# A decayed linear attention and a maxout feed-forward: from nested periods to one written list of steps

## The chip, the cores and the metric

The kernel runs on one core of a Trainium2 chip. Its engines are TensorE (PE; its weight loads are a row of their own, PEld), VectorE (DVE), ScalarE (ACT), GpSimd (POOL) and SyncE (SP), which here only issues DMAs. Each engine takes its instructions in the order in which the program writes them. The metric is the device time of one execution in microseconds, as the median of several runs.

## What is computed

An attention with a state that decays per channel (`S` is 768 steps, 8 heads of 48 channels, batch 4), and then a feed-forward whose hidden value is the larger of two projections (width 1024):

```python
for t in range(S):
    cur = einsum('bhd,bhe->bhde', u * k[t], v[t])
    y[t] = einsum('bhd,bhde->bhe', r[t], state + cur)
    state = w[t][..., None] * state + einsum('bhd,bhe->bhde', k[t], v[t])
x = y.transpose(0, 2, 1, 3).reshape(B * S, H * D)
out = np.maximum(x @ w1, x @ w2) @ w_out
```

The term of `cur` is called the bonus here: for each step and head it is v times the sum of r·k·u over the channels.

## The kernel before

The sequence is cut into six chunks of 128 steps, and a unit is one chunk of two batch entries (called halves, b = 0 and 1): 12 units in all, `units` in line 41, with the two pairs of batch entries in turn. A unit depends on the state that the same pair left a chunk earlier, two units before.

Attention of a unit: `log_w` (L122) takes the logarithm of w on ACT, `excl` (L132) sums it along the chunk on TensorE with a triangular matrix, and `incl` (L133, VectorE), `Aex` (L137, ACT) and `Ainv` (L164, ACT) are made from that sum. `scaled_r` and `scaled_k` (L168, L171, VectorE) multiply r and k with them. `transposes` (L198) turn both on TensorE into one PSUM tile `tp`, copied out by ACT for half 0 and by VectorE for half 1 (L206, L208); `scores` (L217) multiplies them into `mt_p`, and `mask` (L222, VectorE) takes the triangle into `MTm`. `y_sum` adds the part from the state (L236) and that of the chunk (L240) to the tile `y_p`.

The bonus goes ahead of that: `bonus_k` (L175, GpSimd) makes k·u, `bonus_r` (L181, VectorE) multiplies by r, `bonus_sum` (L185, VectorE) reduces to `dg`, and `bonus_out` (L229, VectorE) writes v·dg into `y_p`, for each half, before the matmuls that add to it. One matmul at the start (L85) marks the tile so that all later ones add. There is one `y_p`, one `ex_p`, one `tp` and one `mt_p` (two banks); `kv_p` and the transposed x share a bank, and the feed-forward has two. After `y_sum`, ACT copies out `xs` (L246), `x_transposes` (L253) turns it, VectorE copies `xT` (L257). The state is added up by `state_sum` (L268), `state_out` (L277, L279 on VectorE, L284 on GpSimd), with a decay that goes through DRAM (`row` L143, back as `Wt` L150, exponential `Wx` L159).

Feed-forward: the larger of a and b is half of (a + b) plus half of |a − b|. So the weights are prepared once: the difference w1 − w2 (`wd_sb`, L323, VectorE), the sum (L322, GpSimd), which is transposed (L328) and multiplied with w_out (`prep_product`, L334). `hidden` (L295) multiplies x with the difference in four steps of six matmuls, and ACT takes the absolute value (L298); `rows_out` adds x times the product (L304, three matmuls) and the absolute value times w_out (L308, eight) for each half, and `store` copies out and stores (L314, L316).

The order is written by hand. `start()` runs attention 0, the preparation and hidden 0; then `period(i, j, f, more)` interleaves attention of unit i, the preparation of r and k of unit j = i + 1, the feed-forward of unit f = i − 1, and the loads of unit i + 2. All DMAs go through SP's queue: four loads of 384 KB a unit (w, k, r, v; three buffers each), two weight loads of 512 KB for each of three row blocks, w_out, u, the decay's row and the stores.

Of the kernel before, what the change touches and what calls it, by code (L numbers as in the profile page):

```python
# [12 lines left out]
AX = mybir.AxisListType  # L13


@with_exitstack
def kernel(
# [77 lines left out]
    wof = const.tile([C, FO, HD], F32)  # L95

    def load_w12():
        for ko in range(KO):
            nc.sync.dma_start(out=w1f[:, ko, :], in_=moe_w1[ko * C:(ko + 1) * C, :])
            nc.sync.dma_start(out=w2f[:, ko, :], in_=moe_w2[ko * C:(ko + 1) * C, :])  # L100

    def load_wo():
        nc.sync.dma_start(out=wof, in_=moe_w_out.rearrange("(o p) n -> p o n", p=C))

    def load(i):
        c, bp = units[i]
        sl = bass.ds(c * C, C)
        t = {}
        for name, src in (("w", w), ("k", k), ("r", r), ("v", v)):
# [20 lines left out]
    def excl(i, b):  # L130
        ex_p = ps.tile([C, HD], F32, tag="ex")
        nc.tensor.matmul(ex_p, triU, flat(st[i]["lw"][:, b]))  # L132
        nc.vector.tensor_add(flat(st[i]["incl"][:, b]), ex_p, flat(st[i]["lw"][:, b]))  # L133
        st[i]["ex", b] = ex_p

    def a_excl(i, b):
        nc.scalar.activation(flat(st[i]["Aex"][:, b]), st[i].pop(("ex", b)), AF.Exp)  # L137

    def chunk_decay_row(i):
        if units[i][0] == NC - 1:  # L140
            return
        row = dram.tile([1, NB * HD], F32)
        nc.sync.dma_start(out=row, in_=st[i]["incl"][C - 1:C].rearrange("o b h d -> o (b h d)"))  # L143
        st[i]["row"] = row

    def chunk_decay(i):
        if units[i][0] == NC - 1:
            return
        for ab in range(2):
# [5 lines left out]
    def chunk_decay_exp(i):
        if units[i][0] == NC - 1:
            return
        Wx = work.tile([C, NB, PR], F32)
        nc.scalar.activation(Wx, Wts[i % 2], AF.Exp)  # L159
        st[i]["Wx"] = Wx  # L160

    def a_inv(i):
        Ainv = work.tile([C, NB, H, D], F32)
        nc.scalar.activation(Ainv, st[i]["incl"], AF.Exp, scale=-1.0)  # L164
        st[i]["Ainv"] = Ainv

    def scaled_r(i):
        nc.vector.tensor_mul(rps[i % 2][:, :, :, 0:D], tiles[i]["r"], st[i]["Aex"])  # L168

    def scaled_k(i):  # L170
        nc.vector.tensor_mul(kps[i % 2][:, :, :, 0:D], tiles[i]["k"], st[i]["Ainv"])  # L171

    def bonus_k(i):
        ku = work.tile([C, NB, HD], F32)
        nc.gpsimd.tensor_mul(ku, tiles[i]["k"].rearrange("p b h d -> p b (h d)"),  # L175
                             u_b.unsqueeze(1).to_broadcast([C, NB, HD]))
        st[i]["ku"] = ku

    def bonus_r(i):
        ku = st[i]["ku"]  # L180
        nc.vector.tensor_mul(ku, tiles[i]["r"].rearrange("p b h d -> p b (h d)"), ku)  # L181

    def bonus_sum(i):
        dg = work.tile([C, NB * H, 1], F32)
        nc.vector.reduce_sum(dg, st[i]["ku"].rearrange("p b (h d) -> p (b h) d", d=D), axis=AX.X)  # L185
        st[i]["dg"] = dg

    def cast_v(i):
        vb = work.tile([C, NB, H, D], BF16)
        nc.gpsimd.tensor_copy(vb, tiles[i]["v"])  # L190
        st[i]["vb"] = vb


    def transposes(i, b):
        tp = ps.tile([C, 2, PR, C], BF16, tag="tp")
# [5 lines left out]
        st[i]["tp", b] = tp  # L201

    def transposes_out(i, b):
        rkT = work.tile([C, 2, PR, C], BF16, bufs=3)
        if b == 0:
            nc.scalar.copy(rkT, st[i].pop(("tp", b)))  # L206
        else:
            nc.vector.tensor_copy(rkT, st[i].pop(("tp", b)))  # L208
        st[i]["rkT", b] = rkT

    def scores(i, b):
        rkT = st[i]["rkT", b]
        mt_p = ps.tile([C, 2, PR, C], F32, tag="mt")
# [4 lines left out]
        st[i]["mt", b] = mt_p  # L218

    def mask(i, b):  # L220
        MTm = work.tile([C, 2, PR, C], BF16, bufs=3)
        nc.vector.tensor_mul(  # L222
            MTm.rearrange("p a q c -> p (a q) c"),
            st[i].pop(("mt", b)).rearrange("p a q c -> p (a q) c"),
            triU.unsqueeze(1).to_broadcast([C, H, C]))
        st[i]["MTm", b] = MTm

    def bonus_out(i, b):
        nc.vector.tensor_mul(y_p.rearrange("p (h d) -> p h d", d=D), tiles[i]["v"][:, b],  # L229
                             st[i]["dg"][:, b * H:(b + 1) * H].to_broadcast([C, H, D]))  # L230

    def y_sum(i, b):
        c, bp = units[i]
        if c > 0:
            for p in range(PR):
                nc.tensor.matmul(y_p[:, 2 * p * D:2 * (p + 1) * D], st[i]["rkT", b][:, 0, p, :],  # L236
                                 S_z[bp][:, b, p].rearrange("p a d -> p (a d)"),
                                 start=False, stop=False, skip_group_check=True)
        for h in range(H):
            nc.tensor.matmul(y_p[:, h * D:(h + 1) * D], st[i]["MTm", b][:, h % 2, h // 2, :],  # L240
                             st[i]["vb"][:, b, h, :], start=False, stop=(h == H - 1),
                             skip_group_check=True)

    def y_out(i, b):
        xs = work.tile([C, HD], BF16, bufs=3)
        nc.scalar.copy(xs, y_p)  # L246
        st[i]["xs", b] = xs

    def x_transposes(i, b):
        if b == 0:  # L250
            st[i]["xt"] = ps.tile([C, KO, NB, C], BF16, tag="kv", name="xt_p")
        for j in range(KO):
            nc.tensor.transpose(st[i]["xt"][:, j, b, :], st[i]["xs", b][:, j * C:(j + 1) * C], ident)  # L253

    def x_out(i):
        xT = mlp.tile([C, KO, NB, C], BF16, bufs=3)
        nc.vector.tensor_copy(xT, st[i].pop("xt"))  # L257
        st[i]["xT"] = xT

    def state_sum(i):  # L260
        if units[i][0] == NC - 1:
            return
        kv_p = ps.tile([C, NB, PR, D], F32, tag="kv")
        for b in range(NB):
            for p in range(PR):
                for a in range(2):
                    h = 2 * p + a
                    nc.tensor.matmul(kv_p[a * DP:(a + 1) * DP, b, p, :], kps[i % 2][:, b, h, :],  # L268
                                     st[i]["vb"][:, b, h, :])
# [17 lines left out]
    def hidden(i, f2):  # L287
        xT = st[i]["xT"]
# [231 lines left out]
```

## Time and profile before

| what | us |
|---|---|
| median of 3 runs (182.97 to 183.9) | 183.27 |
| the profiled execution | 183.35 |
| its span in the profile | 181.6 |
| ACT busy | 95.0 |
| GpSimd busy | 65.7 |
| GpSimd waiting for k to land | 40.7 |

Idle time on an engine that isn't the bottleneck costs nothing, and the busy time of TensorE counts pipelined matmuls, so that a row near 100% isn't yet an engine at its peak. A group's row gives its count, then its busy time and the mean duration of one in ns, then the idle time ahead of it and what ended that. "93.25 0.66 PE g_p L295 x6" in the chain is start, duration and what, merged over six instructions.

### The profile page before, as it was taken

Reading aid. Unit: us, or ns where it says so; the run is one execution under the profiler, and the core shown is the slowest. Engines: PE = TensorE matmul, PEld = TensorE weight load, DVE = VectorE, ACT = ScalarE, POOL = GpSimd, SP = SyncE. Lnnn points to the kernel's source line nnn. Section 1 sums busy time; section 2 is a strip of 40 time slices with the busy share of each in tenths; the row PEclk is TensorE's granted clock in tenths of the full one; section 3 lists DMA queues with packets and bytes.
Section 4 is the critical chain, followed back from the end, with each engine's and each line's share of the span. In section 5 each row is a group of like instructions: output and inputs, shape, how many; then the busy total and the mean of one; then the engine's idle time right before and its main releaser. Section 6 shows DMA issues by size and latency. Waiting matters only on the chain.

```text
span 181.6 us, 3831 instructions
## 1 busy us (share of the span) xinstructions
PE 151.1 (83%) x1537; PEld 101.8 (56%) x1537; DVE 130.1 (72%) x172; ACT 95.0 (52%) x171; POOL 65.7 (36%) x63
## 2 busy tenths in 40 slices
PE   0643376997677799999999999999999999999992
PEld 0212274554444467666667676666666766767661
DVE  2157896568389869979799797997979979747100
ACT  2222153555523474746847478465685656655351
POOL 8219914108344305054450454505545145000000
PEclk9999999999699699999999999999999999999999
DMA  5979999979929805968949779597795981020112
GB/s 116 234 251 418 379 210 178 196 147 166 185 44 214 178 4 112 224 147 175 220 96 230 157 141 226 120 224 168 144 213 118 207 191 50 0 90 0 44 46 87
DMA packets 112614, 28.82 MB, mean 159 GB/s; under 512 B 107594, under 2 KB 111818, under 8 KB 112596
## 3 DMA queue, kind: packets, MB, share of 16 engines
q1 hardware_dynamic: 112596, 28.58, 71.0%
q8 instruction: 12, 0.20, 0.5%
q14 instruction: 6, 0.05, 0.1%
HBM read 23.82 MB, written 4.75 MB: 157 GB/s over the span
## 4 chain that ended last, share of the span: by engine, by line
PE 55%; DVE 25%; issue 6%; ACT 4%; DMA 4%; SPq 3%; POOL 1%; ACTq 0%; DVEq 0%; POOLq 0%
PE o_p L308 14%; PE ex_p L132 8%; PE g_p L295 8%; DVE MTm L222 8%; PE o_p L304 6%; DVE y_p L229 5%; PE mt_p L217 4%; DMA u_b<-in_u_dram 4%; DVE ku L181 3%; PE tp L198 3%; SPq L111 3%; PE y_p L236 3%; PE y_p L240 3%; PE wc_p L334 2%; PE kv_p L268 2%
## 5 line engine op out<-in xcount | busy, mean ns | idle before, releaser
L175 POOL TENSOR_TENSOR ku<-kt,u_b 128x768 f32<-128x768 f32 x12 | 24.4, 2031 | 48.2 <-DMA kt<-in_k_dram 40.7
L295 PE MATMUL g_p<-xT,wd_sb 128*128 128x256 bf16 x288 | 40.9, 282 | 0.0
L308 PE MATMUL o_p<-wo_sb,gT 128*128 128x384 bf16 x192 | 37.9, 332 | 0.0
L298 ACT ACTIVATE gT<-g_p 128x512 bf16<-128x512 f32 x48 | 28.5, 597 | 8.9 <-PE g_p L295 8.3
L222 DVE TENSOR_TENSOR MTm<-mt_p,triU 128x1024 bf16<-128x1024 f32 x24 | 29.3, 1220 | 4.8 <-PE mt_p L217 4.3
L132 PE MATMUL ex_p<-lw,triU 128*128 128x384 f32 x48 | 23.3, 571 | 10.2 <-ACT lw L122 6.4
L284 POOL CAST sz<-sf 48x384 bf16<-48x384 f32 x20 | 18.0, 898 | 35.8 <-DVE sf L279 32.8
L295 PEld LDWEIGHTS <-wd_sb 128*128 128x128 bf16 x288 | 26.8, 100 | 5.6 <-issue 1.4
L314 ACT COPY osb<-o_p 128x384 f32<-128x384 f32 x24 | 11.5, 479 | 30.6 <-PE o_p L308 30.6
L308 PEld LDWEIGHTS <-gT 128*128 128x128 bf16 x192 | 18.7, 100 | 11.7 <-issue 1.0
L133 DVE TENSOR_TENSOR incl<-ex_p,lw 128x384 f32<-128x384 f32 x24 | 13.2, 550 | 12.1 <-PE ex_p L132 12.1
L246 ACT CAST xs<-y_p 128x384 bf16<-128x384 f32 x24 | 11.5, 480 | 19.3 <-PE y_p L240 12.9
L137 ACT ACTIVATE Aex<-ex_p 128x384 f32<-128x384 f32 x24 | 11.8, 493 | 16.6 <-DVE incl L133 16.6
L257 DVE COPY xT<-xt_p 128x768 bf16<-128x768 bf16 x12 | 6.7, 557 | 15.0 <-PE xt_p L253 15.0
L304 PE MATMUL o_p<-wc_sb,xT 128*128 128x384 bf16 x72 | 16.2, 334 | 0.0
L181 DVE TENSOR_TENSOR ku<-rt,ku 128x768 f32<-128x768 f32 x12 | 14.5, 1204 | 2.0 <-POOL ku L175 2.0
L132 PEld LDWEIGHTS ex_p<-lw,triU 128*128 128x128 f32 x48 | 7.8, 205 | 14.3 <-ACT Aex L137 7.5
L240 PE MATMUL y_p<-vb,MTm 128*128 128x48 bf16 x192 | 9.2, 188 | 7.5 <-DVE MTm L222 4.0
L229 DVE TENSOR_TENSOR y_p<-vt,dg 128x384 f32<-128x384 f32 x24 | 15.2, 635 | 0.1
L206 ACT COPY rkT<-tp 128x1024 bf16<-128x1024 bf16 x12 | 12.1, 1012 | 3.2 <-PE tp L198 3.2
L240 PEld LDWEIGHTS <-MTm 128*128 128x128 bf16 x192 | 7.6, 99 | 8.5 <-DVE MTm L222 6.8
L198 PE MATMUL tp<-ident,rp 128*128 128x128 bf16 x96 | 9.8, 228 | 2.5 <-DVE rp L168 2.5
(49 smaller groups left out, 205.6 us busy)
## 6 DMA issues: line engine op xcount, KB each, us to landing
wt<-in_w_dram SPq DMA_DIRECT2D x12, 384.0 KB
kt<-in_k_dram SPq DMA_DIRECT2D x12, 384.0 KB
rt<-in_r_dram SPq DMA_DIRECT2D x12, 384.0 KB
vt<-in_v_dram SPq DMA_DIRECT2D x12, 384.0 KB
out_dram<-osb SPq DMA_DIRECT2D x24, 192.0 KB
w1f<-in_moe_w_dram SPq DMA_DIRECT2D x3, 512.0 KB
w2f<-in_moe_w_dram SPq DMA_DIRECT2D x3, 512.0 KB
wof<-in_moe_w_out_dram SPq DMA_DIRECT2D x1, 1536.0 KB
```

What stands on the lines that cost most here:

```text
L132: nc.tensor.matmul(ex_p, triU, flat(st[i]["lw"][:, b]))
L175: nc.gpsimd.tensor_mul(ku, tiles[i]["k"].rearrange("p b h d -> p b (h d)"), u_b.unsqueeze(1).to_broadcast([C, NB, HD]))
L181: nc.vector.tensor_mul(ku, tiles[i]["r"].rearrange("p b h d -> p b (h d)"), ku)
L198: nc.tensor.transpose(tp[:, q, p, :], src[:, b, 2 * p:2 * p + 2, :].rearrange("p h d -> p (h d)"), ident)
L222: nc.vector.tensor_mul(MTm.rearrange("p a q c -> p (a q) c"), st[i].pop(("mt", b)).rearrange("p a q c -> p (a q) c"), triU.unsqueeze(1).to ...
L229: nc.vector.tensor_mul(y_p.rearrange("p (h d) -> p h d", d=D), tiles[i]["v"][:, b], st[i]["dg"][:, b * H:(b + 1) * H].to_broadcast([C, H, D]))
L240: nc.tensor.matmul(y_p[:, h * D:(h + 1) * D], st[i]["MTm", b][:, h % 2, h // 2, :], st[i]["vb"][:, b, h, :], start=False, stop=(h == H - 1 ...
L284: nc.gpsimd.tensor_copy(S_z[bp][rows, :, :, a, :], S_f[bp][rows])
L295: nc.tensor.matmul(g_p[:, q, :], wd_sb[:, ko, fo * C:(fo + 1) * C], xT[:, ko].rearrange("p b c -> p (b c)"), start=(ko == 0), stop=(ko == ...
L298: nc.scalar.activation(st[i]["gT"][:, f2 * 2:f2 * 2 + 2, :], g_p, AF.Abs)
L304: nc.tensor.matmul(st[i]["o", b], st[i]["xT"][:, ko, b, :], wc_sb[:, ko, :], start=(ko == 0), stop=False)
L308: nc.tensor.matmul(st[i]["o", b], st[i]["gT"][:, fo, b * C:(b + 1) * C], wo_sb[:, fo, :], start=False, stop=(fo == FO - 1))
```

## The change

The two functions `start` and `period` give way to one string, `ORDER`, of steps for the whole program. A step is a name with the unit and, where there is one, the half or part: `T.3.1` is the transposes of unit 3, half 1. A short loop calls the function of each step in turn, so the string is the order of every engine's queue at once. The names: `ld*` loads (`ldw12` a block of w1 and w2, `ldwo` w_out), `lw ex incl aex ainv` the decay, `rp kp` scaled r and k, `T TO` transposes and their copy out, `M MO` scores and mask, `Y YO` the sum and its copy out, `X XO` x transposed and copied, `K sa sm sb` the state, `row wt wx` its decay, `H HO` hidden and its absolute value, `O1 O2 OO st` the output, its copy and the store, `wsum wdif wT wTO wp wpO` the preparation of the weights.

In the list the feed-forward of a unit comes one to two units behind its attention, and prefix sums (`ex`) run up to two units ahead. Input buffers go from three to four, and other buffers grow.

What is computed moves too. `rku` (k·u·r) is on GpSimd instead of VectorE. `bv` (v times dg) is made on GpSimd in SBUF, and `YO` on VectorE adds it where y leaves PSUM, in place of ACT's copy; the sum in PSUM starts without the bonus and without the seeding matmul. `XO`, the copy of the transposed x, goes from VectorE to ACT. w_out is loaded by a DMA on GpSimd's queue that converts to bfloat16 on the way, in place of a load on SP's and a scaling on ACT; the half goes into `HO` and `wpO`. The first state is copied instead of added to a cleared tile.

```diff
+ORDER = """
+ldw.0 ldw.1 ldk.0 ldu ldr.0 ldw12.2 ldv.0 ldw12.0 lw.0 ex.0.0 incl.0.0 aex.0.0 ex.0.1 incl.0.1 ainv.0 row.0
+ldw.2 ldw12.1 ldr.1 ldk.1 ku.0 aex.0.1 kp.0 lw.1 ex.1.0 rp.0 rku.0 T.0.0 TO.0.0 wsum.2 aex.1.0 M.0.0 T.0.1
+MO.0.0 TO.0.1 vb.0 dg.0 M.0.1 Y.0.0 wT.2 incl.1.0 bv.0 MO.0.1 ex.1.1 wdif.2 wsum.0 YO.0.0 lw.2 wdif.0 X.0.0
+Y.0.1 aex.1.1 incl.1.1 ldwo YO.0.1 row.1 ldv.1 ldw.3 wt.0 wdif.1 ldk.2 X.0.1 ldr.2 wsum.1 ex.2.0 ldw.4 XO.0
+wT.0 wTO.2 aex.2.0 ainv.1 wTO.0 H.0.0 incl.2.0 H.0.1 HO.0.0 rp.1 K.0 HO.0.1 H.0.2 kp.1 ku.1 wT.1 HO.0.2 ex.2.1
+sa.0 T.1.0 wTO.1 H.0.3 rku.1 TO.1.0 incl.2.1 wp.0 wt.1 row.2 ldv.2 ldk.3 HO.0.3 ldr.3 T.1.1 wpO.0 dg.1 M.1.0
+aex.2.1 vb.1 wp.2 MO.1.0 bv.1 K.1 wpO.2 wp.1 sa.1 lw.3 TO.1.1 ainv.2 Y.1.0 ex.3.0 YO.1.0 wpO.1 aex.3.0
+incl.3.0 X.1.0 M.1.1 ku.2 wx.0 kp.2 O1.0.0 MO.1.1 O2.0.0 rku.2 ex.3.1 sm.0 OO.0.0 Y.1.1 rp.2 aex.3.1 O1.0.1
...
+Y.5.1 OO.3.0 ex.8.0 row.7 wx.4 st.2.0 YO.5.1 st.2.1 ldk.8 H.4.0 ldv.7 ldr.8 rku.6 OO.3.1 T.6.0 incl.8.0 wt.6
+st.3.0 HO.4.0 X.5.0 st.3.1 sm.4 H.4.1 TO.6.0 X.5.1 H.4.2 HO.4.1 dg.6 M.6.0 vb.6 HO.4.2 T.6.1 aex.8.0 MO.6.0
+H.4.3 sb.4 XO.5 ex.8.1 HO.4.3 TO.6.1 H.5.0 incl.8.1 bv.6 H.5.1 HO.5.0 M.6.1 HO.5.1 H.5.2 MO.6.1 aex.8.1 Y.6.0
...
+H.9.3 HO.9.2 bv.11 sm.9 M.11.0 HO.9.3 O1.9.0 MO.11.0 vb.11 O1.9.1 TO.11.1 sb.9 O2.9.0 X.10.1 M.11.1 OO.9.0
+O2.9.1 XO.10 st.9.0 Y.11.0 OO.9.1 H.10.0 YO.11.0 st.9.1 H.10.1 MO.11.1 HO.10.0 X.11.0 HO.10.1 H.10.2 Y.11.1
+HO.10.2 H.10.3 YO.11.1 O1.10.0 HO.10.3 X.11.1 O2.10.0 XO.11 O1.10.1 OO.10.0 st.10.0 O2.10.1 H.11.0 OO.10.1
+st.10.1 H.11.1 HO.11.0 H.11.2 HO.11.1 H.11.3 HO.11.2 O1.11.0 HO.11.3 O2.11.0 O1.11.1 OO.11.0 st.11.0 O2.11.1
+OO.11.1 st.11.1
+"""
...
-    inp = tc.alloc_tile_pool(name="inp", bufs=3)
+    inp = tc.alloc_tile_pool(name="inp", bufs=4)
     work = tc.alloc_tile_pool(name="wrk", bufs=2)
-    mlp = tc.alloc_tile_pool(name="mlp", bufs=2)
+    mlp = tc.alloc_tile_pool(name="mlp", bufs=3)
...
-    y_p = ps.tile([C, HD], F32)
-    nc.tensor.matmul(y_p, ident, S_z[0].rearrange("p b q a d -> p (b q a d)")[:, 0:HD])
...
+    def ldwo():
+        nc.gpsimd.dma_start(out=wo_sb, in_=moe_w_out.rearrange("(o p) n -> p o n", p=C))
...
+    def wpO(ko):
+        nc.scalar.mul(wc_sb[:, ko, :], st.pop(("wp", ko)), 0.5)
...
-    def bonus_r(i):
-        ku = st[i]["ku"]
-        nc.vector.tensor_mul(ku, tiles[i]["r"].rearrange("p b h d -> p b (h d)"), ku)
...
+    def rku(i):
+        nc.gpsimd.tensor_mul(st["ku", i], st["r", i].rearrange("p b h d -> p b (h d)"), st["ku", i])
...
+    def bv(i):
+        x = work.tile([C, NB, HD], F32, tag="bv", name="bv")
+        nc.gpsimd.tensor_mul(x.rearrange("p b (h d) -> p (b h) d", d=D),
+                             st["v", i].rearrange("p b h d -> p (b h) d"),
+                             st["dg", i].to_broadcast([C, NB * H, D]))
+        st["bv", i] = x
...
-    def bonus_out(i, b):
-        nc.vector.tensor_mul(y_p.rearrange("p (h d) -> p h d", d=D), tiles[i]["v"][:, b],
-                             st[i]["dg"][:, b * H:(b + 1) * H].to_broadcast([C, H, D]))
...
+        y_p = ps.tile([C, HD], F32, tag="y", name="y_p")
         for h in range(H):
+            nc.tensor.matmul(y_p[:, h * D:(h + 1) * D], st["MTm", i, b][:, h % 2, h // 2, :],
+                             st["vb", i][:, b, h, :], start=(h == 0), stop=(c == 0),
                              skip_group_check=True)
...
-    def y_out(i, b):
-        xs = work.tile([C, HD], BF16, bufs=3)
-        nc.scalar.copy(xs, y_p)
...
+    def YO(i, b):
+        x = work.tile([C, HD], BF16, tag="xs", name="xs", bufs=4)
+        nc.vector.tensor_add(x, st.pop(("y", i, b)), st["bv", i][:, b])
+        st["xs", i, b] = x
...
+    def XO(i):
+        x = mlp.tile([C, KO, NB, C], BF16, tag="xT", name="xT", bufs=8)
+        nc.scalar.copy(x, st.pop(("xt", i)))
...
+        if c == 0:
+            nc.vector.tensor_copy(x, kv)
+        else:
+            nc.vector.tensor_add(x, kv, x)
...
+    def HO(i, f2):
+        nc.scalar.activation(st["gT", i][:, f2 * 2:f2 * 2 + 2, :], st.pop(("g", i, f2)), AF.Abs, scale=0.5)
...
     with tc.manual_schedule():
-        start()
-        for i in range(1, n + 1):
-            period(i if i < n else None, i + 1 if i + 1 < n else None, i - 1,
-                   i + 2 if i + 2 < n else None)
+        for step in ORDER.split():
+            name, *at = step.split(".")
+            ops[name](*(int(x) for x in at))
```

More of the change, by code (lines that the diff above doesn't have):

```diff
@@ L57 @@
     u_b = const.tile([C, HD], F32)
-    rps, kps = [], []
+    rps, kps, Wts = [], [], []
     for i in range(2):
@@ L94 @@
     w2f = const.tile([C, KO, d_ff], F32)
[L95 to L109, printed above, removed]
+    st = {}
@@ L130, in excl @@
[L130 to L149, printed above, removed]
+                out=x, in_=src[bp * NB:(bp + 1) * NB, :, c * C:(c + 1) * C, :].rearrange("b h s d -> s b h d"))
+            st[name, i] = x
+        return fn
+    def lw(i):
+        x = work.tile([C, NB, H, D], F32, tag="lw", name="lw")
+        nc.scalar.activation(x, st["w", i], AF.Ln)
+        st["lw", i] = x
+    def ex(i, b):
+        ex_p = ps.tile([C, HD], F32, tag="ex", name="ex_p")
+        nc.tensor.matmul(ex_p, triU, flat(st["lw", i][:, b]))
+        st["ex", i, b] = ex_p
@@ L153, in chunk_decay @@
                 allow_slow_non_contiguous=True)
[L155 to L168, printed above, removed]
@@ L225, in mask @@
             triU.unsqueeze(1).to_broadcast([C, H, C]))
-        st[i]["MTm", b] = MTm
-    def bonus_out(i, b):
-        nc.vector.tensor_mul(y_p.rearrange("p (h d) -> p h d", d=D), tiles[i]["v"][:, b],
-                             st[i]["dg"][:, b * H:(b + 1) * H].to_broadcast([C, H, D]))
-    def y_sum(i, b):
-        c, bp = units[i]
[L234 to L238, printed above, removed]
+        st["MTm", i, b] = x
```

409 lines of the change are left out of this document (164 added, 245 removed).

## The prediction

> **What bounds it now.** I read the page first, then the stretches, then the chain in order of time. The page:
>
> ```profile
> span 181.6 us, 3831 instructions
> PE 151.1 (83%) x1537; PEld 101.8 (56%) x1537; DVE 130.1 (72%) x172; ACT 95.0 (52%) x171; POOL 65.7 (36%) x63
> PE   0643376997677799999999999999999999999992
> GB/s 116 234 251 418 379 210 178 196 147 166 185 44 214 178 4 112 224 147 175 220 96 230 157 141 226 120 224 168 144 213 118 207 191 50 0 90 0 44 46 87
> ```
>
> The PE digits are 9 from slice 16 on and 3 to 7 before it. The average of 83% is two regimes, so I cut the span at the starts of the periods:
>
> ```profile
> core 0: us, PE busy (x) PEld busy (x) DVE busy (x) ACT busy (x) POOL busy (x), PEclk, DMA share, GB/s
> 0.00:13.00 13.00, 4.24 (x10) 1.55 (x11) 3.91 (x6) 3.84 (x5) 5.04 (x16) 1.00 0.85 190
> 13.00:30.00 17.00, 8.14 (x93) 6.61 (x94) 14.02 (x14) 5.37 (x5) 12.58 (x6) 1.00 1.04 320
> 30.00:44.70 14.70, 13.08 (x87) 7.74 (x85) 8.54 (x14) 7.59 (x15) 4.06 (x6) 1.00 0.87 160
> 44.70:57.60 12.90, 10.36 (x98) 6.26 (x98) 8.83 (x12) 5.45 (x10) 6.13 (x5) 0.87 0.73 145
> 57.60:69.60 12.00, 9.58 (x94) 6.14 (x92) 9.53 (x14) 5.36 (x11) 1.93 (x2) 0.86 0.52 111
> 69.60:81.30 11.70, 11.43 (x132) 7.95 (x131) 10.40 (x15) 7.42 (x14) 4.76 (x5) 1.00 0.83 171
> 138.70:150.20 11.50, 11.29 (x132) 7.81 (x130) 10.26 (x15) 7.42 (x14) 4.78 (x5) 1.00 0.84 174
> ```
>
> From 81.3 us on a period takes 11.5 us, with TensorE busy 11.29 and VectorE 10.26: there is little to win. Before 81.3, TensorE was busy 4.24 + 8.14 + 13.08 + 10.36 + 9.58 + 11.43 = 56.8 us; 24.5 us were idle. Why it starts so late stands in the chain (start, duration, what):
>
> ```profile
> 6.26 6.66 DMA u_b<-in_u_dram
> 13.06 1.81 POOL ku L175
> 14.90 1.55 DVE ku L181
> ...
> 17.47 1.60 DVE y_p L229
> ...
> 29.52 1.41 PE g_p L295 x6
> ...
> 35.96 4.07 PE wc_p L334 x24
> ```
>
> The bonus of unit 0 sits ahead of its first output sum: u lands, GpSimd multiplies, VectorE multiplies, reduces and writes y_p, and only then may TensorE add to it. The feed-forward of unit 0 starts at 29.5.
>
> **Part by part: TensorE's work and the early stage (A).** The matmuls stay as they are, except that the seeding one goes. What they cost once warm, in the same chain:
>
> ```profile
> 24.52 0.87 PE tp L328 x8
> ...
> 93.25 0.66 PE g_p L295 x6
> 93.91 0.65 PE ex_p L132 x2
> ...
> 100.03 0.49 PE o_p L304 x3
> ...
> 103.01 1.30 PE o_p L308 x8
> ```
>
> A unit's feed-forward is 4 × 0.66 + 2 × (0.49 + 1.30) = 6.2 us; the rest of the 11.29, attention, is 5.1. By 81.3 the kernel has done feed-forward 0 to 2 (18.6), attention 0 to 3 (20.4), the prefix sums of unit 4 (2 × 0.65 = 1.3), three weight transposes (2.6) and three products (4.1): 47.0 us. Stage A asks when the new list has done as much.
>
> Its hidden sums of unit 0 need all w1 and w2. Ahead of the last block SP issues six 393 KB tensors, u and two more blocks, with that block 5.7 MB. By the GB/s digits (4.54 us each) the old kernel had moved 4.6 MB at 18.2 us and 6.35 MB at 22.7, so 21 to 23 us; some five more for VectorE's difference of the last block, what stands ahead of it in its queue and the copy of x put H.0.0 at about 28, against 29.5. By then the list has placed attention 0 without its state sum (4.7), the prefix sums of unit 1 and half of unit 2 (1.95) and two weight transposes (1.7): 8.4 us. Of 47.0, 38.6 are left. At the share of the old steady period (11.29/11.5 = 0.98) they take 39.4 us and A ends at 67.4; at that of 30.0 to 81.3 (44.45 of 51.3, or 0.87) 44.4 us and 72.4. I take **70, so 11.3 us off**: feed-forward may now fill attention's waits, but single units still make up the first ten microseconds of it.
>
> Can the loads keep up? The landings of the old kernel show where GpSimd waited for them:
>
> ```profile
> 27.92 2.12 POOL L175 TENSOR_TENSOR ku<-kt,u_b 128x768 f32<-128x768 f32 x1 [4.36 <-DMA kt<-in_k_dram]
> 31.98 0.82 POOL L190 CAST vb<-vt 128x768 bf16<-128x768 f32 x1 [1.94 <-DMA vt<-in_v_dram]
> 46.70 1.81 POOL L175 TENSOR_TENSOR ku<-kt,u_b 128x768 f32<-128x768 f32 x1 [1.41 <-DMA kt<-in_k_dram]
> ```
>
> v of unit 1 lands at 32, k of unit 3 at 46.7: 8 to 10 us a unit, and a period moves a unit's loads and stores in a DMA share of 0.84 of 11.5 = 9.7 us. So v arrives about 33, 43, 52 and 62 for units 1 to 4. Attention 3 has to be through at 70, so loads are ahead by ten microseconds. On SP, stores wait for their output copy and loads queue behind them, as before; four input buffers instead of three give a unit more of slack. I cost that at nothing; uncovered, a late load costs TensorE its own lateness.
>
> w_out now comes from GpSimd's queue, converted on the way, and ACT loses its conversion. No such DMA is in the trace. GpSimd issues it behind ku, k·u·r, the bonus (2.03 each, by ku's row below), two weight sums (7.97 for three) and the cast (0.82) of unit 0: 12.2 us after u, which now has three tensors ahead of it instead of four and lands near 11. That and a wait or two make it 25. At the 400 GB/s of slices 4 and 5 its 1.57 MB take 4 us, at half of that 8: landed at 29 to 34. wp.0 stands behind T.1.0 and H.0.3, not before 33. I take it as hidden; if it is late, everything on PE stands behind wp.0. The Trainium skill, "DMA: Bandwidth & Descriptors", section "SWDGE vs HWDGE vs iDMA", adds that VectorE can hold up the building of such descriptors; no run here shows it yet.
>
> **The other engines in the steady stage (B).** The groups, with count, busy time and mean in ns:
>
> ```profile
> L229 DVE TENSOR_TENSOR y_p<-vt,dg 128x384 f32<-128x384 f32 x24 | 15.2, 635 | 0.1
> L181 DVE TENSOR_TENSOR ku<-rt,ku 128x768 f32<-128x768 f32 x12 | 14.5, 1204 | 2.0 <-POOL ku L175 2.0
> L257 DVE COPY xT<-xt_p 128x768 bf16<-128x768 bf16 x12 | 6.7, 557 | 15.0 <-PE xt_p L253 15.0
> L133 DVE TENSOR_TENSOR incl<-ex_p,lw 128x384 f32<-128x384 f32 x24 | 13.2, 550 | 12.1 <-PE ex_p L132 12.1
> L246 ACT CAST xs<-y_p 128x384 bf16<-128x384 f32 x24 | 11.5, 480 | 19.3 <-PE y_p L240 12.9 <-DVE rkT L208 6.2
> L206 ACT COPY rkT<-tp 128x1024 bf16<-128x1024 bf16 x12 | 12.1, 1012 | 3.2 <-PE tp L198 3.2
> L175 POOL TENSOR_TENSOR ku<-kt,u_b 128x768 f32<-128x768 f32 x12 | 24.4, 2031 | 48.2 <-DMA kt<-in_k_dram 40.7
> ```
>
> VectorE loses ku·r (1.20), two bonus writes (2 × 0.64) and the x copy (0.56), and gains YO twice, a PSUM operand plus an SBUF one like incl (2 × 0.55): 10.26 − 3.03 + 1.10 = 8.3 us a period. ACT loses xs (2 × 0.48) and gains the x copy (1.01 × 768/1024 = 0.76): 7.2. GpSimd gains two products like ku (2 × 2.03): 8.8. Only TensorE stays near 11.
>
> What it waits for in six steady periods, 81.3 to 150.2 (total, times, longest):
>
> ```profile
> PEld L236 <- issue: 3.6, 12, 0.4
> PEld L217 <- ACT rkT L206: 3.3, 6, 0.5
> PEld L268 <- issue: 1.9, 6, 0.3
> PEld ex_p L132 <- ACT Aex L137: 1.6, 5, 0.5
> ```
>
> The weight loader's 10.4 us are 1.7 a period; the matmul row has 0.2 idle. A reordering can win between 0.2 and 1.7 a period, and lose through GpSimd, because the two engines get in each other's way:
>
> ```profile
> 15.59 7.97 POOL L322 TENSOR_TENSOR ws_sb<-w1f,w2f 128x1024 bf16<-128x1024 f32 x3
> ...
> 22.64 1.35 DVE L229 TENSOR_TENSOR y_p<-vt,dg 128x384 f32<-128x384 f32 x1
> ...
> L229 DVE TENSOR_TENSOR y_p<-vt,dg x24: 554/559/1603, 17.5 to 166.7; 128x384 f32<-128x384 f32 x24
> ```
>
> y_p, 0.56 in the median (the last row: shortest, median, longest), took 1.35 from 22.64, to the end of GpSimd's sums (23.56) and its own time more. With GpSimd busy 8.8 of 11.5 = 0.77, an operation of two SBUF operands (rp, kp and sm: three a unit) would meet one running and wait on average half of 2.03: 3 × 0.77 × 1.0 = 2.3 us, and VectorE comes to 10.6. That still is below 11.29, but not idle enough to forgive much. I take **0.5 a period, six periods, 3.0 us off** (bounds 10 off, 4 on), and nothing for the last three periods, where the last unit's feed-forward still stands alone.
>
> The Trainium skill, "SBUF — State Buffer", section "Who interferes with whom", says the pair of ports is a lock: the second one "fully blocks". The trace agrees (22.64 to 23.56); by that rule the move of k·u·r to GpSimd costs VectorE time elsewhere, and the sum would be the forecast's or, if every meeting is lost whole, the slower rival's.
>
> **Sum.** The profiled execution took 183.35 us (span 181.6), against a median of 183.27. 183.35 − 11.3 − 3.0 = **169.0 us**.
>
> **Rivals.** *Dense*: TensorE waits for nothing once warm; A ends at 67.4 (−13.9) and B wins 1.3 a period (−8): 161.4. For it: every other engine is below 9 us a unit by its rows; against it: in-order queues and one buffer each for ex, y and mt. *w_out late*: a descriptor-built load under VectorE's stream lands ten microseconds after wp.0 is due; A wins 1.3 and B 3: 179. Against it: 1.57 MB is 4 to 8 us. *Slower, the lock*: each rp, kp and sm loses a whole GpSimd operation, 3 × 2.03 = 6.1; VectorE then needs 14.4 a unit, 2.9 over the period, for eight periods: +23, which with A's −11.3 gives 195. It decides once VectorE passes 11.5 + 11.3/8 = 12.9, that is 1.5 us lost per operation. Against it: y_p has two SBUF operands too, and over all 24 its mean of 0.64 is only 0.08 above its median, with GpSimd busy 4.78 of 11.5.
>
> **How the numbers follow.** Forecast 0.60, dense 0.20, w_out late 0.12, slower 0.08. The range of 160 to 179 takes in A from 67.4 to 72.4, B's bounds and the first two rivals; what is left out is the lock and the far ends. 0.5%, or 0.9 us, is what a measurement can tell from no change here: faster 0.90, same 0.02, slower 0.08.
>
> **What would show it.** A right: H.0.0 at 28 and TensorE's digits at 9 from slice 7 or 8 instead of 16. B right: a steady period near 11.0, VectorE near 10 with rp, kp and sm above 0.95, 0.95 and 0.56. Wrong: wp.0 waiting for w_out, TensorE waiting for MTm, rkT or xs with VectorE over 11, or loads that land after their unit is due.

## The result and the profile after

The changed kernel takes 170.81 us in the median of four runs (170.04 to 171.58) against 183.42: a ratio of 0.931, with a 95% interval of 0.926 to 0.937. The forecast was 169.0, with 160 to 179. Where 14.3 us were expected, 12.6 came. Ratios go by the faster runs of both kernels alone, which for the kernel before lie at 183 to 184 us here and from 179.9 us up in the later series, so the repeat below has 0.944 at the same median. Span and work in the page's lines:

```profile
span 169.8 us, 3790 instructions
PE 145.7 (86%) x1536; PEld 100.1 (59%) x1536; DVE 125.7 (74%) x148; ACT 90.6 (53%) x158; POOL 104.0 (61%) x86
PE   0435573599999989998999999999999999999991
GB/s 123 202 235 331 282 299 102 210 187 211 180 105 93 198 177 191 145 132 226 235 131 232 216 222 152 223 205 185 300 221 82 144 0 93 50 42 53 64 35 93
PE 67%; DVE 18%; issue 5%; DMA 4%; ACT 4%; DVEq 0%; ACTq 0%
```

TensorE's digits reach 9 in slice 8 (34 us) instead of 16, as forecast, but the slices before it are no better than they were. The load of w_out, now on GpSimd's queue, took 7.6 us, and GpSimd's busy time went from 65.7 to 104.0. Cut into stretches (length, then busy time and count of each engine, granted clock, DMA share, GB/s):

```profile
0.00:13.00 13.00, 3.75 (x5) 1.49 (x6) 3.70 (x6) 4.57 (x6) 6.81 (x16) 1.00 0.88 190
13.00:28.00 15.00, 7.87 (x63) 4.52 (x62) 12.08 (x13) 2.74 (x4) 12.16 (x7) 1.00 1.02 269
28.00:40.00 12.00, 9.82 (x71) 6.92 (x72) 9.75 (x11) 4.20 (x7) 6.85 (x4) 1.00 1.16 187
40.00:50.00 10.00, 10.00 (x103) 5.90 (x101) 6.55 (x10) 5.74 (x12) 5.07 (x3) 1.00 0.95 171
50.00:60.00 10.00, 9.53 (x109) 6.58 (x107) 8.94 (x10) 7.45 (x14) 8.09 (x6) 1.00 0.74 134
...
75.00:105.00 30.00, 29.27 (x348) 20.84 (x346) 27.39 (x37) 21.18 (x39) 21.33 (x18) 1.00 1.08 206
```

From 40 us on TensorE is nearly full until the tail (9.53 us of the ten from 50 to 60). The waits of its matmul row and the longest of its weight loader between 45 and 160 us say how full (total, times, longest):

```profile
PE tp L270 <- DVE rp L234: 1.4, 2, 0.7
PE tp L270 <- DVE kp L237: 0.3, 1, 0.3
PE mt_p L289 <- DVE rkT L280: 0.2, 1, 0.2
PEld L289 <- issue: 3.3, 10, 0.5
PEld L270 <- DVE rp L234: 2.6, 3, 1.3
```

In 115 us the matmul row waited 1.9 us for other engines, and what the loader waited for most is rp, a product of VectorE. No row of rp stood among the waits of the steady stage before.

**Where the 11.8 us of the span came from.** The marks are the first hidden sums of a unit: H.0.0 started at 29.5 before and starts at 32.92 now, and H.3.0, which opened the steady stage at 81.6, starts at 77.2. At that point the list is ahead in attention: beyond what stage A asks for, it has done the prefix sums of unit 5 and half of unit 6 (1.95 us), the transposes of unit 4 (0.90), half of its scores (0.33) and one of its sums (about 0.4), 3.6 us in all. So stage A ended near 73.6 instead of 81.3: 7.7 us. The rest, from there to the end, is 169.8 − 73.6 = 96.2 against 100.3: 4.1 us. All of A's gain came after 33 us; up to there the new kernel is the slower one. The same count at H.9.0 (150.5 before, 144.2 now) finds the list ahead by the transposes of units 10 and 11, the prefix sums of 11, the scores and one sum of 10, about 4.2 us, so the six periods that ended at 150.2 now end near 140.0. They take 66.4 us instead of 68.9: about 2.5 of the 4.1 us lie there and 1.6 in the tail.

Part of the 7.7 us may be the clock's. The granted clock was 0.87 and 0.86 in the two stretches of before from 44.7 to 69.6 us, and 1.00 in every stretch of the new trace. Four matmuls of one kind, in that time and after it, in the kernel before:

```profile
48.12 1.48 PE L308 MATMUL o_p<-wo_sb,gT 128*128 128x384 bf16 x4
...
78.16 0.81 PE L308 MATMUL o_p<-wo_sb,gT 128*128 128x384 bf16 x4
```

At 1.00 the 10.36 and 9.58 us that TensorE was busy in the two stretches would be 10.36 × 0.87 + 9.58 × 0.86 = 17.3 instead of 19.9: by this estimate up to 2.7 of the 7.7 us. No run holds the clock fixed, and why it fell is not shown.

### The profile page after: what moved, and what is told of

Same layout as the page of the kernel before. It is cut to its first block, busy times and chain, and to the rows that moved or that the text cites. A ratio compares the mean times of both kernels' runs of the same rounds, so it can differ in the third digit from the quotient of the medians.

```text
span 169.8 us, 3790 instructions
## 1 busy us (share of the span) xinstructions
PE 145.7 (86%) x1536; PEld 100.1 (59%) x1536; DVE 125.7 (74%) x148; ACT 90.6 (53%) x158; POOL 104.0 (61%) x86
## 4 chain that ended last, share of the span: by engine, by line
PE 67%; DVE 18%; issue 5%; DMA 4%; ACT 4%; DVEq 0%; ACTq 0%
PE o_p L378 17%; PE g_p L368 14%; PE ex_p L198 8%; PE tp L270 7%; PE o_p L384 6%; DVE rp L234 5%; PE mt_p L289 4%; DVE MTm L294 4%; PE y_p L305 2%; PE wc_p L174 2%; DVE wd_sb L160 2%; DMA wt<-in_w_dram 2%; PE xt_p L323 2%; DVE kp L237 2%; DMA Wt<-row 2%
## 5 line engine op out<-in xcount | busy, mean ns | idle before, releaser
L368 PE MATMUL g_p<-xT,wd_sb 128*128 128x256 bf16 x288 | 39.1, 282 | 2.1 <-DVE wsT_sb L169 2.1
L255 POOL TENSOR_TENSOR bv<-vt,dg 128x768 f32<-128x768 f32 x12 | 17.7, 1473 | 15.7 <-DVE dg L250 11.2
L358 POOL CAST sz<-sf 48x384 bf16<-48x384 f32 x20 | 13.4, 672 | 22.0 <-DVE sf L351 21.4
L241 POOL TENSOR_TENSOR ku<-kt,u_b 128x768 f32<-128x768 f32 x12 | 23.0, 1920 | 5.7 <-DMA u_b<-in_u_dram 5.5
L246 POOL TENSOR_TENSOR ku<-rt,ku 128x768 f32<-128x768 f32 x12 | 24.4, 2034 | 0.8
L209 ACT ACTIVATE Aex<-ex_p 128x384 f32<-128x384 f32 x24 | 11.8, 491 | 14.3 <-DVE incl L204 7.4
L234 DVE TENSOR_TENSOR rp<-rt,Aex 128x768 bf16<-128x768 f32 x12 | 19.3, 1608 | 0.0
L393 ACT COPY osb<-o_p 128x384 f32<-128x384 f32 x24 | 11.5, 482 | 14.0 <-PE o_p L378 12.2
L316 DVE TENSOR_TENSOR xs<-y_p,bv 128x384 bf16<-128x384 f32 x24 | 13.2, 549 | 6.0 <-PE y_p L309 5.5
L237 DVE TENSOR_TENSOR kp<-kt,Ainv 128x768 bf16<-128x768 f32 x12 | 15.6, 1303 | 1.1 <-ACT Ainv L213 1.1
L327 ACT COPY xT<-xt_p 128x768 bf16<-128x768 bf16 x12 | 9.6, 800 | 8.2 <-PE xt_p L323 8.2
L262 POOL CAST vb<-vt 128x768 bf16<-128x768 f32 x12 | 12.6, 1046 | 1.6 <-DMA vt<-in_v_dram 1.4
```

The lines of the kernel that those rows point to most:

```text
L234: nc.vector.tensor_mul(rps[i % 2][:, :, :, 0:D], st["r", i], st["Aex", i])
L237: nc.vector.tensor_mul(kps[i % 2][:, :, :, 0:D], st["k", i], st["Ainv", i])
L241: nc.gpsimd.tensor_mul(x, st["k", i].rearrange("p b h d -> p b (h d)"), u_b.unsqueeze(1).to_broadcast([C, NB, HD]))
L246: nc.gpsimd.tensor_mul(st["ku", i], st["r", i].rearrange("p b h d -> p b (h d)"), st["ku", i])
L255: nc.gpsimd.tensor_mul(x.rearrange("p b (h d) -> p (b h) d", d=D), st["v", i].rearrange("p b h d -> p (b h) d"), st["dg", i].to_broadcast( ...
L358: nc.gpsimd.tensor_copy(S_z[bp][rows, :, :, a, :], S_f[bp][rows])
```

## The experiments

Times are medians. The kernel before is timed beside each series of runs; in the later series its own runs lie between 179.9 and 185.3 us, so a ratio is given with its interval. Edits worth 1 or 2 us are read in us against the kernel after, whose ten runs in two series lie between 168.75 and 171.7 with a median of 170.7: one such edit alone is hardly clear of that spread.

| kernel | us | ratio to before | interval |
|---|---|---|---|
| after | 170.81 | 0.931 | 0.926 to 0.937 |
| the same once more | 170.69 | 0.944 | 0.937 to 0.951 |
| old order, moved work, as it stood | 198.21 | 1.096 | 1.085 to 1.107 |
| old order, moved work, mended | 183.87 | 1.016 | 1.008 to 1.025 |
| new order, work where it was | 178.16 | 0.984 | 0.976 to 0.992 |
| k·u·r on VectorE | 168.62 | 0.925 | 0.915 to 0.934 |
| the same once more | 168.76 | 0.928 | 0.919 to 0.936 |
| k·u·r on VectorE for units 0 and 1 | 169.19 | 0.936 | 0.930 to 0.942 |
| k·u·r of unit 0 later | 169.50 | 0.939 | 0.933 to 0.944 |
| w_out's load between GpSimd's products | 169.90 | 0.943 | 0.937 to 0.949 |
| that, and k·u·r on VectorE | 169.83 | 0.941 | 0.934 to 0.949 |
| three input buffers | 170.50 | 0.944 | 0.937 to 0.952 |
| one GpSimd product more a unit | 173.81 | 0.963 | 0.957 to 0.969 |

### Order and moved work, one without the other

The change does two things at once, so the four corners were made: the theory was that the order is the gain. First the functions of the kernel after, in the order of the kernel before:

```diff
 ORDER = """
-ldw.0 ldw.1 ldk.0 ldu ldr.0 ldw12.2 ldv.0 ldw12.0 lw.0 ex.0.0 incl.0.0 aex.0.0 ex.0.1 incl.0.1 ainv.0 row.0
+ldw.0 ldk.0 ldr.0 ldv.0 ldu ldw12.0 ldw12.1 ldw12.2 lw.0 ex.0.0 incl.0.0 aex.0.0 ex.0.1 incl.0.1 aex.0.1 ainv.0
...
```

> The functions of the kernel after, called in the order of the kernel before (its start and periods written out as a list; w_out on GpSimd's queue, k*u*r and the bonus on GpSimd, bonus added at the PSUM read). Theory 'order': the gain is the order's; the moved operations only relieve VectorE (about 8.3 us busy a period instead of 10.3), and a period that TensorE already fills for 11.29 of 11.5 us stays near 11.3: 179 to 182 us, feed-forward of unit 0 from 29 to 31 us. Rival 'moved work': a freer VectorE and no bonus ahead of the sums is what made it faster: 174 us or less with the old order.

It took 198.2 us, slower than both: a miss for both theories. Its waits tell why:

```profile
ACT Aex L210 <- DVE incl L205: 42.0, 24, 6.1
POOL sz L359 <- DVE sf L352: 40.6, 10, 7.3
DVE dg L251 <- POOL ku L247: 35.9, 11, 5.3
```

The old order asks for the sum over the channels (dg) right behind k·u·r. With that product on GpSimd, VectorE stood before dg for 35.9 us, with the prefix sums queued behind it. So the position was mended: k·u·r behind k·u, dg and the bonus late in the period.

```diff
-T.2.0 TO.2.0 rku.3 dg.3 bv.3 H.1.0 HO.1.0 ex.3.0 incl.3.0 aex.3.0
+T.2.0 TO.2.0 H.1.0 HO.1.0 ex.3.0 incl.3.0 aex.3.0
...
-Y.2.1 YO.2.1
+Y.2.1 YO.2.1 dg.3 bv.3
...
-lw.4 ku.4
+lw.4 ku.4 rku.4
```

> The old order with the moved work once more, now with k*u*r right behind k*u on GpSimd, and its sum over the channels and the bonus late in the period, so that VectorE no longer stands 3 us before that sum ahead of the prefix sums. Theory 'the old order with the moved work lost only by that wait': 3.1 us less in each of ten periods where it was on the path, but a period does not fall under 11.2: 180 to 184 us. Rival 'the moves themselves cost': still over 190.

183.87: about the upper end. The moved work alone, decently placed, is slower than before by a ratio of 1.016. TensorE was busy 29.26 of 30 us between 75 and 105, no less than in the periods before (11.29 of 11.5). Nor did VectorE come out freer: it was busy 133.1 us in all, against 130.1 before, since kp and the decay of the state took two to three times the 0.95 and 0.54 us that they take at their shortest:

```profile
L238 DVE TENSOR_TENSOR kp<-kt,Ainv 128x768 bf16<-128x768 f32 x12 | 23.9, 1990 | 0.5 <-ACT Ainv L214 0.5
L352 DVE TENSOR_TENSOR sf<-sf,Wx 128x384 f32<-128x384 f32 x10 | 14.5, 1454 | 2.4 <-ACT Wx L231 1.4
```

So this corner moved work off VectorE and gave the time back. The rows point to meetings with GpSimd, whose ku and bonus took 2.37 and 2.01 us there instead of 1.81 and 1.47.

The other corner keeps the list and puts the work back (the bonus written into PSUM by VectorE behind the mask of its half, k·u·r and the copy of x on VectorE, the copy of y on ScalarE; w_out's load and the buffers stay as in the kernel after):

```diff
-    def bv(i):
...
+    def BO(i, b):
+        nc.vector.tensor_mul(y_p.rearrange("p (h d) -> p h d", d=D), st["v", i][:, b],
+                             st["dg", i][:, b * H:(b + 1) * H].to_broadcast([C, H, D]))
...
-        nc.vector.tensor_add(x, st.pop(("y", i, b)), st["bv", i][:, b])
+        nc.scalar.copy(x, y_p)
...
-        nc.gpsimd.tensor_mul(st["ku", i], st["r", i].rearrange("p b h d -> p b (h d)"), st["ku", i])
+        nc.vector.tensor_mul(st["ku", i], st["r", i].rearrange("p b h d -> p b (h d)"), st["ku", i])
```

> The new list with the work where it was: the bonus written into PSUM by VectorE ahead of the sums (each write placed right behind the mask of its half), k*u*r on VectorE, the copy of y on ScalarE, the copy of x on VectorE, one seeded tile for y; w_out's load and the buffers as after. Theory 'the order alone is the gain': 168 to 173 us, like the kernel after. Rival 'order and moves need each other': VectorE is back at 10.3 to 11 us a unit in a list that fills TensorE for 11, and waits of TensorE for VectorE come back: 176 to 182 us.

178.16: the rival was right. The waits of the matmul row between 45 and 160 us:

```profile
PE tp L271 <- DVE rp L238: 3.0, 2, 2.3
PE y_all L304 <- DVE y_all L258: 2.8, 4, 1.2
PE ex_p L202 <- ACT Aex L213: 1.1, 1, 1.1
PE ex_p L202 <- DVE incl L208: 1.1, 1, 1.1
```

And the same stretch as above, to be held against 29.27 busy there:

```profile
75.00:105.00 30.00, 26.07 (x317) 18.18 (x315) 27.22 (x39) 18.93 (x37) 8.13 (x8) 1.00 1.01 197
```

TensorE is busy 26.07 of 30 us. It waits for rp, for the bonus (`y_all`) and for incl, which are VectorE's, and once for Aex of ScalarE. By the ratios of one series the order alone saves 1.6%, the moved work alone costs 1.6%, and both together save 5.6%: hardly any of the gain is the sum of the two.

The traces say where each of the two counts. With the moved work left out the list reaches H.3.0 as early as with it, the steps ahead of it being the same but for the bonus (first the list with the old work, then the kernel after):

```profile
77.14 0.82 PE L366 MATMUL g_p<-xT,wd_sb 128*128 128x256 bf16 x6
...
77.16 0.82 PE L368 MATMUL g_p<-xT,wd_sb 128*128 128x256 bf16 x6
```

So the 7.7 us of stage A are the order's. (The moved work is the later one at H.0.0, 32.92 against 29.33 with the old work, and has made that good by H.3.0.) From H.3.0 to the end the old work takes 176.6 − 77.1 = 99.5 us and the moved work 169.8 − 77.2 = 92.6. Those 6.9 us are what the moves are worth in this list, and its waits above say by which engine: without the moves VectorE holds TensorE up, and the list loses part of what it won early. A little of it may again be the clock, which was 0.94 between 105 and 135 us in that run.

### What held the first forty microseconds

H.0.0 came at 32.9 where 28 was forecast. VectorE's line and GpSimd's between 27 and 32 us of the kernel after (start, duration, engine, line, operation), and H.0.0 itself with the wait ahead of it:

```profile
27.97 4.29 DVE L160 TENSOR_TENSOR wd_sb<-w1f,w2f 128x1024 bf16<-128x1024 f32 x1
...
27.05 2.36 POOL L157 TENSOR_TENSOR ws_sb<-w1f,w2f 128x1024 bf16<-128x1024 f32 x1
29.36 1.81 POOL L241 TENSOR_TENSOR ku<-kt,u_b 128x768 f32<-128x768 f32 x1
31.25 2.68 POOL L246 TENSOR_TENSOR ku<-rt,ku 128x768 f32<-128x768 f32 x1
...
32.92 1.46 PE L368 MATMUL g_p<-xT,wd_sb 128*128 128x256 bf16 x6 [2.07 <-DVE wsT_sb L169]
```

H.0.0 needs the last weight difference, and what released it was a copy that stood behind that difference in VectorE's queue. The difference, 1.21 us by itself, took 4.29: it met the weight sum, was passed over when GpSimd went on with k·u at once, and got in at the small gap ahead of k·u·r, which waited in its turn (2.68 instead of 1.81). The Trainium skill, "SBUF — State Buffer", section "Who interferes with whom", calls the ports that VectorE and GpSimd share an exclusive lock and says that the one to issue first gets the pair and the other "fully blocks"; the trace agrees (the difference, begun at 27.97, waited for the sum that ended at 29.41), and adds that whoever waits can lose the next turn too, here to k·u, which began later. Two lists with one step moved test it. The first is about the earliest meeting, that of rp of unit 0, which took 2.55 us, with k·u·r:

```diff
-ku.0 aex.0.1 kp.0 lw.1 ex.1.0 rp.0 rku.0 T.0.0 TO.0.0 wsum.2 aex.1.0
+ku.0 aex.0.1 kp.0 lw.1 ex.1.0 rp.0 T.0.0 TO.0.0 wsum.2 rku.0 aex.1.0
```

> The new list with one step moved: k*u*r of unit 0 behind the weight sum wsum.2 on GpSimd, so that GpSimd waits for w1 and w2 when rp of unit 0 comes up. If the lock by GpSimd is what makes that rp 2.55 us, it becomes about 1 us and the transposes of unit 0 start at 14.0 instead of 15.6 us. On the time: 0 to 1.5 us faster, since VectorE's weight differences and not this chain hold the feed-forward. If rp is slow for another reason, rp stays above 2 us.

The first rp took 0.95 instead of 2.55 us and the transposes began at 13.92; 169.5 us, 1.2 below the kernel after. Both as expected. The second puts a step between the weight sum and k·u:

```diff
-aex.1.1 incl.1.1 ldwo YO.0.1 row.1 ldv.1 ldw.3 wt.0 wdif.1 ldk.2 X.0.1 ldr.2 wsum.1 ex.2.0
+aex.1.1 incl.1.1 YO.0.1 row.1 ldv.1 ldw.3 wt.0 wdif.1 ldk.2 X.0.1 ldr.2 wsum.1 ldwo ex.2.0
```

> The new list with one step moved: the issue of w_out's load on GpSimd stands between wsum.1 and ku.1 instead of ahead of wsum.1. Theory 'starved between GpSimd's operations': wdif.1, which took 4.29 us through wsum.1 and ku.1, gets its turn at the end of wsum.1 and is over about 2.7 us earlier; H.0.0 starts at 30 to 30.5 us instead of 32.9, and the time is 2 to 2.5 us lower, 168.3 to 168.8. w_out lands 2.4 us later, at 36, still ahead of the first product at 38 to 40. Rival 'loads set the first forty microseconds': H.0.0 may move, but the time stays at 170.8 since attention 1 and 2 wait for their loads.

Half a hit. The difference took 2.43 us and H.0.0 started at 30.84, but the time is 169.9, 0.8 below the kernel after instead of 2 to 2.5. The step behind the weight sum let VectorE in; the next line shows what it cost:

```profile
38.33 1.47 PE L175 MATMUL wc_p<-wo_sb,wsT_sb 128*128 128x384 bf16 x8 [1.46 <-DMA wo_sb<-in_moe_w_out_dram]
```

w_out, issued 3.1 us later, took 9.2 us instead of 7.6, and TensorE stood before it for 1.46. The wait was moved. In the kernel after itself the load landed at 26.0 + 7.6 = 33.6, well ahead of its first product at 40.07.

### How much of it is GpSimd's product

k·u·r of unit 0 is what the first rp had to wait for. Here k·u·r goes back to VectorE, for all units:

```diff
-        nc.gpsimd.tensor_mul(st["ku", i], st["r", i].rearrange("p b h d -> p b (h d)"), st["ku", i])
+        nc.vector.tensor_mul(st["ku", i], st["r", i].rearrange("p b h d -> p b (h d)"), st["ku", i])
```

> The new list with k*u*r back on VectorE, all else as after. Theory 'the meetings of VectorE with GpSimd cost time early and are covered later': the first rp falls from 2.55 to about 1 us, GpSimd loses 1.9 us a unit and VectorE gains 0.95 to 1.3 but gets some back from shorter rp and kp; the time stays within 1.5 us of 170.8. Rival 'the meetings set the steady stage': at least 3 us faster (167.5 or less). Rival 'VectorE is the bound': at least 3 us slower, since it has one operation more.

168.62 us, with runs from 166.4 to 170.6: 2 us below the kernel after, outside the 1.5 that was named and short of the rivals' 3. The first rp took 0.94 us and H.0.0 started at 29.55. VectorE does one operation more a unit, and the kernel isn't slower but faster.

> The kernel after, unchanged, timed beside the next three on the same chip: 170 to 171 us, a ratio of 0.93 to 0.94. It gives the yardstick for edits that are worth 1 or 2 us.

The yardstick: 170.69. In its trace the same program came out 2.9 us shorter than in the first (span 166.9):

```profile
27.82 2.53 DVE L160 TENSOR_TENSOR wd_sb<-w1f,w2f 128x1024 bf16<-128x1024 f32 x1
...
26.90 2.35 POOL L157 TENSOR_TENSOR ws_sb<-w1f,w2f 128x1024 bf16<-128x1024 f32 x1
29.21 2.81 POOL L241 TENSOR_TENSOR ku<-kt,u_b 128x768 f32<-128x768 f32 x1
```

Here VectorE won the turn behind the weight sum, and k·u waited 1.0 us. H.0.0 started at 31.00 instead of 32.92, which is 1.9 of the 2.9 us. Next, k·u·r goes back to VectorE for the first two units only:

```diff
-        nc.gpsimd.tensor_mul(st["ku", i], st["r", i].rearrange("p b h d -> p b (h d)"), st["ku", i])
+        eng = nc.vector if i < 2 else nc.gpsimd
+        eng.tensor_mul(st["ku", i], st["r", i].rearrange("p b h d -> p b (h d)"), st["ku", i])
```

> The new list with k*u*r on VectorE for units 0 and 1 only, on GpSimd for the other ten. With all twelve on VectorE the traced run was 5 us ahead at 45 us of the span and still 5 us ahead at its end. Theory 'the meetings cost only early': two units give all of it, 1.5 to 3 us below the kernel after in the median, and the feed-forward of unit 0 starts near 29.6 us. Rival 'they cost in every period': most of the gain is lost, less than 0.7 us remains.

169.19, 1.5 below the kernel after in the same series, where all twelve gave 2: by the medians most of the gain comes from the first two units. The runs of the two kernels overlap (169.0 to 170.1 against 168.75 to 171.7), so this is likely and not shown. The feed-forward did not start at 29.6 in its trace, though, but at 31.3, since the last weight difference, begun at 26.34, lost its turn once more and took 4.30 us.

> The new list with k*u*r on VectorE, unchanged, beside the others of this call: 167 to 170 us, runs up to 4 us apart, by the time that wdif.1 takes.

168.76, runs from 166.8 to 170.6: as said. Both traces of this kernel (spans 164.6 and 165.9) show the shorter difference of about 2.5 us; no trace of its longer runs was taken. Whether the turn behind the weight sum makes the spread is tested by both edits at once:

```diff
-aex.1.1 incl.1.1 ldwo YO.0.1 row.1 ldv.1 ldw.3 wt.0 wdif.1 ldk.2 X.0.1 ldr.2 wsum.1 ex.2.0
+aex.1.1 incl.1.1 YO.0.1 row.1 ldv.1 ldw.3 wt.0 wdif.1 ldk.2 X.0.1 ldr.2 wsum.1 ldwo ex.2.0
...
-        nc.gpsimd.tensor_mul(st["ku", i], st["r", i].rearrange("p b h d -> p b (h d)"), st["ku", i])
+        nc.vector.tensor_mul(st["ku", i], st["r", i].rearrange("p b h d -> p b (h d)"), st["ku", i])
```

> The new list with k*u*r on VectorE for all units and the issue of w_out's load between wsum.1 and ku.1. In two traces of the kernel after itself the third weight difference took 4.29 and 2.53 us, and the spans were 169.8 and 166.9: who gets the port between wsum.1 and ku.1 is not fixed. Theory 'that race is the spread': with a DMA issue between the two GpSimd products VectorE always gets in, so 166.5 to 168.5 us with a spread of the runs under 1.5 us. Rival: 168.6 us and a spread of 4 us, as with k*u*r on VectorE alone.

A miss: 169.83, 1.1 above k·u·r on VectorE alone in the same series, and TensorE waited 1.68 us for w_out. The runs spread by 1.7 us against 3.8 beside them, above the 1.5 that was named, and it is the fast ones that are gone (the fastest takes 168.9 instead of 166.8). What makes the runs of one program differ is not settled: the turn behind the weight sum differs between traces, and the edit that fixes it brings the wait for w_out with it.

### Room in the steady stage, and the buffers

How near GpSimd is to setting the pace is tested by giving it a product that nobody needs:

```diff
+    spare = const.tile([C, NB, HD], F32, name="spare")
...
+        if i > 1:
+            nc.gpsimd.tensor_mul(spare, st["r", i].rearrange("p b h d -> p b (h d)"), u_b.unsqueeze(1).to_broadcast([C, NB, HD]))
```

> The new list with one more GpSimd product for each of units 2 to 11 (r times u into a tile that nobody reads), 1.8 us a unit. Theory 'the steady stage has room': GpSimd goes to about 10 us a unit and rp and kp lose more, but TensorE's wait stays small: 171 to 173 us. Rival 'GpSimd and the lock already set the pace of the steady stage': ten times 1.8 us, up to 188 us.

173.81: 3.1 us for ten products of 1.8. There is room, though the time lies just above the expected end. GpSimd is now nearly full (27.90 of 30 us between 75 and 105), and TensorE is busy 27.49 there instead of 29.27:

```profile
75.00:105.00 30.00, 27.49 (x328) 19.29 (x326) 27.76 (x32) 19.53 (x36) 27.90 (x18) 1.00 0.99 202
```

The last one takes the fourth input buffer away:

```diff
-    inp = tc.alloc_tile_pool(name="inp", bufs=4)
+    inp = tc.alloc_tile_pool(name="inp", bufs=3)
```

> The new list with three input buffers instead of four. The list issues no load earlier than its buffer of three units before is free by the list, so the time stays at 170 to 171.5 us, as the prediction had it (cost nothing). Rival: SP stands before a used buffer and loads come late: 173 us or more.

170.5: the fourth buffer costs and gives nothing that can be measured.

## Why the prediction was right

**The bound.** Right: TensorE fills the second part, and the idle time to win lay ahead of 81 us. VectorE's share of the chain went from 25% to 18%, TensorE's from 55% to 67%.

**Stage A.** The term was mis-sized: 11.3 us forecast, 7.7 in the first trace, and its end near 73.6 lies outside the bounds of 67.4 to 72.4. The step that failed is "H.0.0 at about 28": it priced VectorE's weight differences and products at their own time and kept the lock for the steady stage. In the runs the first rp took 2.55 us and the last two differences 2.90 and 4.29, and H.0.0 came at 32.9. From there the 38.6 us of work that were left took 40.7, a share of 0.95, inside the 0.87 to 0.98 of the working but above the 0.92 behind its 70: so the 4.9 us late at H.0.0 became 3.6 at A's end.

Two things in that sum were not said. It prices every matmul at the full clock, and so counts as gain, without naming it, what the kernel before lost while its clock was 0.87 and 0.86 (up to 2.7 us by the estimate above). And its 0.87 is a share of busy time, in which the early, slower matmuls count longer (56.8 us busy for 47.0 us of work at the working's own prices), while it is laid on work at warm prices.

**w_out.** Right: landed at 33.6 (29 to 34 was the estimate), hidden until 40.07. Its rival fell for this place in the list, and came true in small in the two lists where the issue moved some 3 us: 1.46 and 1.68 us of waiting.

**Loads.** Right for the buffers, by the run with three. That loads keep up was argued only, but the waits of TensorE between 45 and 160 us name no DMA.

**Stage B.** 3.0 forecast, 4.1 measured. By the count at H.9.0 the six periods gave about 2.5 of the 3.0, and the 1.6 behind them were forecast as nothing: the mechanism was right, and the tail made up for part of what A lacked, which is luck for the total. What lets TensorE fill up shows in the corner with the old work: the bonus and the VectorE operations come off its way.

**The lock.** 2.3 us a unit were forecast for VectorE. The groups after:

```profile
L234 DVE TENSOR_TENSOR rp<-rt,Aex 128x768 bf16<-128x768 f32 x12 | 19.3, 1608 | 0.0
L237 DVE TENSOR_TENSOR kp<-kt,Ainv 128x768 bf16<-128x768 f32 x12 | 15.6, 1303 | 1.1 <-ACT Ainv L213 1.1
L351 DVE TENSOR_TENSOR sf<-sf,Wx 128x384 f32<-128x384 f32 x10 | 8.1, 806 | 0.1
L255 POOL TENSOR_TENSOR bv<-vt,dg 128x768 f32<-128x768 f32 x12 | 17.7, 1473 | 15.7 <-DVE dg L250 11.2 <-DMA kt<-in_k_dram 3.3 <-POOL sz L358 1.0
```

Over their shortest (0.94, 0.95, 0.54) rp, kp and sm lose 0.67, 0.36 and 0.26: 1.3 us a unit. The working took GpSimd as busy 8.8 us a unit; the bonus came out at 1.47 us where ku's 2.03 was used, and GpSimd often idles ahead of it, waiting for dg. The slower rival's point of 1.5 us per operation was reached by single ones (rp of unit 0 lost 1.61), but by no mean; the nearest is kp in the mended old order, which lost 1.04.

**The rivals.** "Dense" was nearly right for B (1.9 us of matmul waits in 115) and wrong for A. What the forecast did not have is the split: it gave the order nearly all of the gain and the moved work the part of a risk. The corners show the order to be right for A, all of whose gain it brings; behind A this list without the moved work is slower than the old order (176.6 − 73.6 = 103.0 us against 100.3), and the moved work costs time without the list.

## What to carry to other kernels

Price an operation that is moved to GpSimd by what it does to VectorE's operations with two operands in SBUF, and price it first where VectorE's chain is the only work there is, at the start. Here the moved work alone cost 1.6% and the new order alone saved 1.6%, against 5.6 to 6.9% for both; where the order can be rewritten, look for the moves that it can use, and try the corners. Here the list with k·u·r back on VectorE is the fastest version measured, 168.6 and 168.8 us in two series. Its ratios to the kernel before, 0.925 (0.915 to 0.934) and 0.928 (0.919 to 0.936), stand beside 0.931 (0.926 to 0.937) and 0.944 (0.937 to 0.951) of the kernel after: the intervals overlap in the first pair and just miss each other in the second, so the 2 us are likely rather than sure.

## What the runs showed of the hardware

A VectorE operation with two SBUF operands that waits for GpSimd does not get the next turn for certain: 4.29 and 2.53 us for the same instruction of the same program in two traces. Operations with a PSUM operand and the sum over channels were untouched throughout, as these views of single lines show (shortest, median, longest in ns):

```profile
L316 DVE TENSOR_TENSOR xs<-y_p,bv x24: 540/548/559, 23.7 to 155.3; 128x384 bf16<-128x384 f32 x24
L250 DVE TENSOR_REDUCE dg<-ku x12: 935/942/953, 20.2 to 146.0; 128x16 f32<-128x768 f32 x12
L255 POOL TENSOR_TENSOR bv<-vt,dg x12: 1466/1474/1476, 21.2 to 147.0; 128x768 f32<-128x768 f32 x12
L234 DVE TENSOR_TENSOR rp<-rt,Aex x12: 942/1642/2553, 13.0 to 137.9; 128x768 bf16<-128x768 f32 x12
```

On GpSimd, the product with a value repeated over 48 channels (bv) took 1.47 us where the one of two full tiles takes 1.81 at its shortest, for the same 768 elements; nothing here tells why.
